# New hand-written order for a chunked recurrence and a gated MLP on one core: narrower unit-matrix products, idle products, and other engines for some pieces

## The chip, the cores and the metric

The kernel runs on one core of one Trainium2 chip. Its time is the device time of one execution in microseconds (us); the time quoted is the median of three runs. Six parts of the core matter: PE (TensorE, the matrix products), PEld (the loading of PE's stationary operand, beside the products), DVE (VectorE), ACT (ScalarE), POOL (GpSimd), and SP, which only issues DMAs. Each works through its own instructions in program order and waits on the others by semaphores.

## The reference

Two parts stand one behind the other. The first is a recurrence over 768 time steps, for 4 batches and 8 heads of width 40:

```
for t in range(S):
    y[:, :, t] = einsum('bhd,bhde->bhe', r_t, state)
    Sa = einsum('bhde,bhe->bhd', state, a_t)
    state = state * w_t - outer(Sa, b_t) + outer(v_t, k_t)
```

The second takes the result as x (4 x 768 x 320) through a gated MLP:

```
h = gelu(x @ w_in)                       # 320 -> 1024
u, v = h[..., :512], h[..., 512:]
v = layernorm(v) * g_ln
v = einsum('ts,bsd->btd', w_sg, v) + b_sg # 768 x 768
out = x + (u * v) @ w_out
```

Everything is in float32; products that need more than one pass split an operand into a high and a low part (names ending in h and l: `vh`, `vl`, `wsh`, `wsl`, `woh`, `wol`, `xh`, `xl`).

## The kernel before

**The recurrence.** The 768 steps are cut into 12 chunks of 64. Inside a chunk the steps are solved together: the decay products and scaled keys are formed for each batch b (the "gates": `ex`, `hs`, `kb`, `at` on DVE and POOL, the products `ab` on PE, the copies `nts`, `kbt`, `at` on ACT), and a triangular system per head pair has to be inverted. The inversion of a chunk is a chain of 58 small operations on POOL (`tg<-x,n`, then `x<-x,tg`), each of which needs the one before. It starts from `n` (a DVE transposition of `nts`) and `x` (an ACT copy of a unit start). Behind it DVE turns the result (`x1z`, later `xt`), PE and ACT finish the inverse (`gp`, `gs`, `xp`), and the chunk's products follow: `ru` (state and right-hand sides), `sp` (the new state), `ut`, `pq` (scores), `yp` (output), which DVE and ACT move on (`rhsb`, `s`, `vu`, `vut`, `vs`, `sc`, `pqs`, `yt`). The chunk's state update `sp` adds the old state through a product with a unit matrix (`sp<-sc,ident`), followed by 16 products of the update itself. The loop runs ahead: while PE works on chunk c, POOL inverts c+1 and the gates of c+2 and c+3 are formed.

For chunk 0 the inversion is divided: DVE does one half of the heads' rows (`tv<-x,n`) and POOL the other (`tg<-x,n`, 15 wide and narrower), both beside the gates of chunk 1.

**The MLP.** Its weights arrive as 64-bit numbers and are taken apart into a high and a low part of 32 bits (`stg`, `lt`, `sc`, then `wih` and `wil`, or `woh` and `wol`): some integer operations on DVE, copies on ACT, and three last operations, "a trio" (`lt<-lt,sc`, `stg<-stg,wih`, `wil<-stg,lt`), on DVE or POOL. The input weights' part of this is laid into the last chunks of the recurrence. Its pieces are named x (load and split of the input, `split_x`), v and u (the two halves of the first product, PE `hv` and `hu`, then a gelu on ACT and DVE and, for v, the norm), s (the product with `w_sg`, PE `sg<-wsh,vh`, `sg<-wsl,vh`, `sg<-wsh,vl`), o (the output product, PE `op`) and j (idle products that nobody reads).

**What sets the order.** Nothing is scheduled by a planner at build time. Every operation goes through `InOrder` (line 146), which pins it to its place in the program, and the places come from tables of numbers at the head of the file. A pair (position, function) is put in a list, the list is sorted by position, and the functions are called in that order: `merge` for chunk 0 and the start of chunk 1, `half` for each half chunk, with 28 units of position to a chunk. The tables that the text below speaks of are `E0K` and `E1K` (one letter for each batch: whether `kb` of chunk 0 and 1 is formed on DVE, V, or on POOL, G), `JUNK` (position and number of idle products in the recurrence), `DEC` (position and engine of the 12 splits of the input weights), `SEQ0`, `SEQ` and `SEQL` (the order of the MLP's pieces), `SGS` and `OUTS` (at which piece each twelfth of `w_sg` and eighth of `w_out` is split), and `SGE` and `OUTE` (on which engine its low part is formed). Since all operations are recorded through `InOrder`, each carries that one line, L156, in the profile; groups are told apart by their tiles.

Of the kernel before, what the change touches and what calls it, by code (L numbers as in the profile page):

```python
# [19 lines left out]
NP = H // 2  # L20
# [16 lines left out]
WARM = (14, 0)  # L37
T0 = 7.22
T1 = 17.01
T2 = 3.25  # L40
TX = 17.22
ISN = 1
LX = 5.0
LV = 9.0
OSP = 1
AQ = 0
YM = 64
C1 = 15.0
WP = 16.0
W16 = 0.42  # L50
K16 = 0
TB0 = 1.08
TB1 = 14.03
CUT0 = ()
HALF = 8
ROWS0 = (6, 31)
T3 = 11.26
T4 = 17.06
CH = ((1.42, 2.46, 7.0, 6.4, 3.47, 7.1, 8.16, 11.36, 3.3, 9.55, 13.14, 14.55), (-0.02, 1.21, 7.67, 4.93, 8.92, 5.92,
    10.0, 10.59, 3.23, 7.11, 13.11, 13.9))  # L60
GPOS = (((0.01, 0.33, 0.61, 1.31, 3.87, 4.25, 4.26, 4.27, 0.611), (2.52, 2.51, 2.79, 3.49, 5.81, 6.43, 6.44, 6.45,
# [10 lines left out]
E1K = "VGGG"
BACK = (17.23, 23.44, 29.46, 23.45)
GX = (24.18, 4.36)
# [17 lines left out]
SEQ0 = (("x0", 0), ("v0", 0), ("v1", 0), ("v2", 0), ("u0", 0), ("x1", 0), ("u3", 0), ("u1", 0), ("u2", 0), ("v3",  # L92
# [4 lines left out]
XL = 2  # L97
REST = 9
SGS = (2, 6, 3, 5, 8, 10, 10, 13, 14, 13, 14, 13)
OUTS = (11, 12, 12, 14, 15, 18, 19, 18)  # L100
XE = "VVVVVVVVVVVV"
UE = "VVVVVVVV"
OSTEP = (-2, 0, 0, 0, 0, 0)
SGE = "VGGGGVGVGVGG"
OUTE = "GGGGGGGG"
SECOND = (17.5, 0.25)
ZERO = (-1, 12.33)
LAST = 2
# [3 lines left out]
MK = 40  # L112
JUNK = ((317.32, 3), (348.72, 4))
TP = 1
UT = 0
GL = (0.01, 0.01)
LAG = ((1.42, 2.31, 0.69, 0.01, 0.01, 1.54, (0.01, 0.69, 0.6, 0.61), (1.29, 1.3, 0.58, 1.19), 2.82, 0.22, 0.11,
    1.02), (0.01, 0.01, 0.88, 0.27, 0.2, 0.01, (0.01, 0.02, 0.35, 0.36), (0.19, 0.3, 0.06, 1.38), 0.01, 0.25, 0.06,
    0.01))
SEQL = ("s1", "s2", "s0", "s3", "s4", "s5", "s6", "s7", "o0", "o1", "o2", "o3", "o5", "o4")  # L120
ROWS = (12, 26)
EX = ((0.01, 0, 0.3, 0.52, 1.42, 2.52, 2.53, 3.02, 0.301), (0.01, 0, 0.3, 0.93, 2.14, 3.24, 3.25, 3.83, 0.54))

# [46 lines left out]
def attention(tc, a, xd, flag, keep, ps, mlp=None):  # L170
# [4 lines left out]
    with ExitStack() as ctx:  # L175
# [463 lines left out]
        def chain3(c, b):  # L639
# [185 lines left out]

        def load_x0():
            Q.dma_start(out=x0, in_=a["x0"])

        def load_v():
            for f in (load_vb, load_vu):  # L830
                for k in range(2):
                    f(0, k)

        bl = blanks()
# [6 lines left out]
              spread(steps16(0, 1, G, K16, 8, "tg"), T3, T4),  # L841
              [(TX + W16 * k, f) for k, f in enumerate(back)], [(LX, load_x0), (LV, load_v)],
              [(C1, lambda: [f() for b in range(2) for f in chain1(0, b)]), (WP, lambda: warmup(WARM[1]))],
# [5 lines left out]

        plan = []  # L850
        for c in range(1, NCH):
# [40 lines left out]
class Mlp:  # L892
# [127 lines left out]

    def weights_rest(self):
        def part_sg(k, c):
# [29 lines left out]
        order = [(k, c) for c in range(2) for k in range(6)]  # L1052
        loads = [lambda x=x: load_sg(*x) for x in order]
        parts = [lambda x=x: part_sg(*x) for x in order]
        wo = [part_out(k, c) for c in range(2) for k in range(4)]
# [108 lines left out]

    def outp(self, b, m, n):
        r = 128 if m < 2 else 64
        mc = slice(128 * m, 128 * m + r)
        self.outs[b, n] = self.outs.get((b, n), 0) + 1
        assert all(("wo", i) in self.ready for i in range(8))
        k = OSP if (b == B - 1 and self.outs[b, n] == 3 and self.outs.get((b, 1 - n)) == 3) else 1  # L1170
        w = 384 // k
        for j in range(k):
            self.outp_part(b, m, n, slice(w * j, w * j + w), w, r, mc)

    def outp_part(self, b, m, n, part, w, r, mc):
        V, Q, sb = self.V, self.Q, self.pr
        c = slice(384 * n + part.start, 384 * n + part.stop)
        o = self.ps("op")[:, 0:w]
        ops = []
        for f in range(4):  # L1180
            h, l = (y[:, part] for y in self.gs[b, f, n])
            if m < 2:
# [18 lines left out]

    def side(self, c, hf):
# [5 lines left out]
        if self.plan is None:  # L1208
# [53 lines left out]
    def run(self, ahead, verdict=None):  # L1262
# [3 lines left out]
        if not ahead:  # L1266
# [143 lines left out]
```

## Time and profile before

| | |
|---|---|
| three runs | 636.78, 638.65, 639.47 us; median 638.65 |
| profiled execution | 635.31 us, span from first to last instruction 633.1 us |
| granted TensorE clock, mean | 0.937 of 2.4 GHz |
| PE busy | 579.1 us, 91% |
| DVE, ACT, POOL busy | 490.2, 392.1, 385.9 us (77%, 62%, 61%) |

The profile's page cuts the span into 40 slices and gives each engine's busy share in tenths, the granted clock and the DMA share:

```profile
PE   6658899999999999999978899598999999999995
DVE  7858788988889888898768778888787769568632
ACT  6928697987978879788765746543454345224410
POOL 7568787888888888888886244566442432343230
PEclk9556699999999999999979899799999999999999
```

A slice is 15.8 us. The recurrence takes the first 24 slices, the MLP the rest. PE is not full in the first five slices, in slices 21 to 23 and in slice 26, and the granted clock is low in about the same places. "Idle before" in a row of the timeline is the time in which the engine had nothing to run, and the name behind the arrow is what it then got.

### The profile page before, as it was taken

How to read it: one execution, taken by the hardware profiler on the slowest of the kernel's cores; microseconds unless marked ns; L12 is line 12 of the kernel's file. 1: busy time of each engine (PE TensorE's matmuls, PEld its weight loads, DVE VectorE, ACT ScalarE, POOL GpSimd, SP SyncE). 2: the span in 40 equal slices, each digit the busy share in tenths (PEclk: the TensorE clock that was granted, in tenths of full speed). 3: DMA queues.
4: the chain of work that ended last, by engine and by line, in shares of the span. 5: the costliest groups of instructions: out<-in, count | busy, mean ns of one | idle time of the engine just before them, and what ended most of it. 6: DMA issues, size and time to landing. Idle time of an engine off the chain costs nothing.

```text
span 633.1 us, 24077 instructions
## 1 busy us (share of the span) xinstructions
PE 579.1 (91%) x9837; PEld 514.9 (81%) x9837; DVE 490.2 (77%) x1074; ACT 392.1 (62%) x1113; POOL 385.9 (61%) x853
## 2 busy tenths in 40 slices
PE   6658899999999999999978899598999999999995
PEld 5556788888888888888867788487899989999995
DVE  7858788988889888898768778888787769568632
ACT  6928697987978879788765746543454345224410
POOL 7568787888888888888886244566442432343230
PEclk9556699999999999999979899799999999999999
DMA  5433233444334444333443325320003103010002
GB/s 197 141 68 94 66 109 105 121 123 124 108 102 123 109 138 108 105 97 94 129 115 101 102 76 170 98 68 10 32 7 100 32 1 107 1 32 14 19 1 68
DMA packets 56887, 54.02 MB, mean 85 GB/s; under 512 B 35840, under 2 KB 47360, under 8 KB 56768
## 3 DMA queue, kind: packets, MB, share of 16 engines
q1 hardware_dynamic: 56768, 52.40, 29.1%
q8 instruction: 79, 1.29, 0.8%
q14 instruction: 40, 0.33, 0.2%
HBM read 44.52 MB, written 7.86 MB: 83 GB/s over the span
## 4 chain that ended last, share of the span: by engine, by line
PE 43%; ACT 21%; DVE 15%; POOL 10%; issue 8%; DMA 2%; SPq 0%; ACTq 0%; POOLq 0%; DVEq 0%
PE sg L156 12%; PE op L156 5%; ACT nts L156 5%; PE hv L156 4%; POOL x L156 4%; POOL tg L156 4%; PE hu L156 4%; PE yp L156 4%; PE ab L156 3%; ACT junk L156 2%; ACT at L156 2%; PE sp L156 2%; PE ru L156 2%; ACT xt L156 2%; PE pq L156 2%
## 5 line engine op out<-in xcount | busy, mean ns | idle before, releaser
L156 POOL TENSOR_TENSOR x<-x,tg 128x126 f32<-128x126 f32 (+24 forms) x334 | 128.5, 385 | 26.1
L156 POOL TENSOR_TENSOR tg<-x,n 128x126 f32<-128x126 f32 (+24 forms) x334 | 122.0, 365 | 32.7 <-ACT x L156 4.0
L156 PE MATMUL sg<-wsh,vh 128*128 128x384 f32 x192 | 66.4, 346 | 4.9 <-ACT vh L156 4.2
L156 POOL TENSOR_TENSOR gx<-g,gy 128x384 fp32r<-128x384 f32 x30 | 32.0, 1073 | 62.7 <-ACT gy L156 62.7
L156 PE MATMUL sg<-wsl,vh 128*128 128x384 f32 x192 | 66.2, 345 | 2.1 <-POOL wsl L156 1.4
L156 PE MATMUL sg<-wsh,vl 128*128 128x384 f32 x192 | 66.1, 344 | 0.8 <-POOL vl L156 0.8
L156 ACT ACTIVATE nts<-ab 32x256 f32<-32x256 f32 x192 | 62.0, 323 | 2.8 <-DVE at L156 0.2
L156 PE MATMUL pq<-rt,vut 128*64 128x128 f32 x768 | 55.7, 289 | 0.2 <-ACT gs L156 0.2
L156 ACT CAST gy<-g 128x384 fp32r<-128x384 f32 x30 | 15.4, 514 | 55.3 <-DVE g L156 52.6
L156 PE MATMUL yp<-pqs,kbt 128*64 128x64 f32 x768 | 46.5, 225 | 2.4 <-DVE pqs L156 0.6
L156 PE MATMUL ab<-at,kb 64*64 64x64 f32 x1536 | 38.8, 243 | 9.9 <-POOL kb L156 4.2
L156 PEld LDWEIGHTS pq<-rt,vut 128*64 128x64 f32 x768 | 44.1, 144 | 3.1 <-DVE lt L156 0.7
L156 ACT CAST vh<-v 128x512 fp32r<-128x512 f32 x24 | 14.9, 620 | 51.2 <-DVE v L156 51.2
L156 PEld LDWEIGHTS ab<-at,kb 64*64 64x64 f32 x1536 | 31.7, 151 | 16.0 <-POOL kbt L156 5.5
L156 POOL TENSOR_TENSOR rs<-rs,mhalf 128x1 f32<-128x1 f32 x24 | 13.7, 571 | 48.6 <-DVE rs L156 40.9
L156 PE MATMUL yp<-rt,s 80*40 80x64 f32 x704 | 42.6, 219 | 0.1
L156 PEld LDWEIGHTS yp<-pqs,kbt 128*64 128x64 f32 x768 | 37.1, 136 | 6.4 <-ACT kbt L156 2.1
L156 PEld LDWEIGHTS sg<-wsh,vh 128*128 128x128 f32 x192 | 37.1, 193 | 6.0 <-ACT vh L156 4.5
L156 POOL TENSOR_TENSOR vl<-v,vh 128x512 fp32r<-128x512 f32 x24 | 31.4, 1311 | 17.3 <-ACT vh L156 17.3
L156 DVE TENSOR_TENSOR pqs<-pq,mask 128x512 f32<-128x512 f32 x48 | 32.0, 682 | 10.1 <-PE pq L156 10.1
L156 PEld LDWEIGHTS sg<-wsl,vh 128*128 128x128 f32 x192 | 37.0, 193 | 3.1 <-POOL wsl L156 1.9
L156 PE MATMUL ru<-rhsb,xt 64*64 64x40 f32 x768 | 32.6, 235 | 7.3 <-ACT xt L156 6.1
(164 smaller groups left out, 1655.4 us busy)
## 6 DMA issues: line engine op xcount, KB each, us to landing
main<-main SPq DMA_DIRECT2D x88, 160.8 KB
vs<-vb SPq DMA_DIRECT2D x24, 160.0 KB
vu<-vs SPq DMA_DIRECT2D x24, 160.0 KB
rt<-rt SPq DMA_DIRECT2D x48, 80.0 KB
vut<-vt SPq DMA_DIRECT2D x24, 160.0 KB
xd<-yt SPq DMA_DIRECT2D x96, 40.0 KB
xt<-xd SPq DMA_DIRECT2D x16, 192.0 KB
out<-y SPq DMA_DIRECT2D x16, 192.0 KB
```

Of the source, the lines that this page charges most:

```text
L156: return self.tc.keep_in_program_order(f(*a, **k))
```

## The change

The file is the same program with other tables and a few other statements:

- The unit-matrix product in `sp` is issued in two parts of 80 columns for each half of the partitions in place of one of 160 (the loop in `chain3`), so 8 instructions in place of 4 for each of the 44 state updates.
- `HEAT` puts 11 products of a constant tile with itself (`wp<-warm`, 128 x 128, 22 instructions) in chunk 0, and `JUNK` has seven entries (29 idle products) in place of two (7). A piece `j6` (six idle products) stands in `SEQ0` ahead of `s1`.
- `wsh` and `wsl` move from the pool `mlp_rest` to a pool of their own, `mlp_sg`, on the other side of the memory, opened at position 313.1. `SGA` is empty, so `early_sg` runs nowhere.
- `E1K` goes from VGGG to GGGV: of chunk 1's four `kb`, the first goes from DVE to POOL and the last from POOL to DVE.
- `SGE` gives DVE six of twelve low parts of `w_sg` in place of four, `OUTE` two of eight of `w_out` in place of none, and `DEC` one more trio of the input weights.
- All other tables have new numbers. The switches `OSP` and `AQ` go; they had the values that leave the program as it is now written. `HALF`, `CUT0` and `ROWS0` are read nowhere.

The core of the difference:

```
-ISN = 1
-E1K = "VGGG"
+E1K = "GGGV"
+HEAT = ((13.17, 11),)
-JUNK = ((317.32, 3), (348.72, 4))
+JUNK = ((294.28, 5), (295.93, 4), (307.25, 6), (312.36, 3), (312.43, 1), (346.91, 3), (349.9, 4))
-SGE = "VGGGGVGVGVGG"
-OUTE = "GGGGGGGG"
+SGE = "GGGGGVGVVVVV"
+OUTE = "VVGGGGGG"
-EARLY = 5
+EARLY = 4
-XL = 2
+XL = 4
-    0), ("v4", 0), ("v5", 0), ("x0", 1), ("u4", 0), ("u6", 0), ("u5", 0), ("u7", 0), ("s1", 0), ("x1", 1), ("s2",
+    0), ("v4", 0), ("v5", 0), ("u4", 0), ("u6", 0), ("u5", 0), ("u7", 0), ("j6", 0), ("s1", 0), ("x0", 1), ("s0",
...
-                w = NP // ISN
-                for g in range(ISN if IS else 0):
+                for g in range(2 if IS else 0):
                     for h in range(2):
                         r = slice(64 * h, 64 * h + 64)
-                        T.matmul(sp[r, w * D * g:w * D * g + w * D], lhsT=ident[:, r],
-                                 rhs=sc[:, w * g:w * g + w].rearrange("p q x -> p (q x)"), start=not g, stop=True,
+                        T.matmul(sp[r, 2 * D * g:2 * D * g + 2 * D], lhsT=ident[:, r],
+                                 rhs=sc[:, 2 * g:2 * g + 2].rearrange("p q x -> p (q x)"), start=not g, stop=True,
...
-        plan = []
+        plan = [(p, lambda k=k: warmup(k)) for p, k in HEAT]
...
+            at(PSG, self.open_sg)
...
     def open_rest(self):
         self.pr = p = self.pool("mlp_rest", "left")
-        self.wsh, self.wsl = (p.tile([128, 6, S], F32R, name=n) for n in ("wsh", "wsl"))
```

What the new numbers move shows best in the instructions of an engine. First POOL at the start of the program, from the last gates of chunk 1 to the first step of chunk 0's inversion (`at_165` and `at_166` belong to batches 2 and 3 of chunk 1). Before:

```order
L156 TENSOR_TENSOR at_165<-main_94,ex_149 128x4x64 [waits DMAHW1_49,DMAHW0_49,DVE_49]
L156 MEMSET kbt_107 128x24
L156 TENSOR_TENSOR kb<-main_94,hs 128x2x4x64 [waits DVE_49,PE_49]
L156 MEMSET kbt_108 128x24
L156 TENSOR_TENSOR at_166<-main_95,ex_150 128x4x64 [waits DMAHW3_49,DMAHW2_49,DVE_49]
L156 MEMSET kbt_109 128x24
L156 TENSOR_TENSOR kb<-main_95,hs 128x2x4x64 [waits DVE_49,PE_49]
L156 MEMSET kbt_110 128x24
```

And in the changed kernel:

```order
L157 TENSOR_TENSOR at_165<-main_94,ex_149 128x4x64 [waits DMAHW1_49,DMAHW0_49,DVE_49]
L157 MEMSET kbt_107 128x24
L157 TENSOR_TENSOR kb<-main_94,hs 128x2x4x64 [waits DVE_49,PE_49]
L157 MEMSET kbt_108 128x24
L157 TENSOR_TENSOR at_166<-main_95,ex_150 128x4x64 [waits DMAHW4_49,DMAHW3_49,DVE_49]
L157 MEMSET kbt_109 128x24
L157 MEMSET kbt_110 128x24
L157 MEMSET kbt_111 128x24
```

The `kb<-main_95,hs` of batch 3 no longer stands between POOL and the chain; DVE has it inside its own half of the inversion (`kb<-main_95,fixed_91`). In exchange POOL has a `kb<-main_92,hs` further up.

Second, PE in chunk 0's second half, at the second `ut` (`ab_1371`, in the changed kernel `ab_1386`, are gate products of chunk 3). Before:

```order
L156 MATMUL sp<-sc_128,ident 64x160 x2
L156 MATMUL sp<-vu_138,kbt_105 40x40 x8
L156 MATMUL ut<-ident,vu_138 80x64 x4
L156 MATMUL ru<-vs_121,at_161 64x40 x8
L156 MATMUL ab_1371<-at_171,kb 64x64
```

And in the changed kernel:

```order
L157 MATMUL sp<-sc_128,ident 64x80 x4
L157 MATMUL sp<-vu_138,kbt_105 40x40 x8
L157 MATMUL ut<-ident,vu_138 80x64 x4
L157 MATMUL wp<-warm 128x128 x11
L157 MATMUL ru<-vs_121,at_161 64x40 x8
L157 MATMUL ab_1386<-at_171,kb 64x64
```

The 11 products stand ahead of the `ru` and of the gate products of chunk 3; the unit-matrix product is twice as many instructions of half the width.

Third, DVE in the first pass of the MLP, between the norms of the last v pieces of batch 0 (`mv`, `rs` are the mean and scale of a norm). Before:

```order
L156 TENSOR_SCALAR v<-v,mv,rs 128x512
L156 BN_AGGR mv<-bs 128x2
L156 TENSOR_SCALAR rs<-mv 128x1
L156 TENSOR_TENSOR xl<-xt_7604,xh 128x384 x2
L156 TENSOR_TENSOR xh<-xt_7604,xh 64x384
L156 SCALAR_TENSOR_TENSOR q<-p,hu 128x384
L156 SCALAR_TENSOR_TENSOR v<-q,hv 128x512
```

And in the changed kernel:

```order
L157 TENSOR_SCALAR v<-v,mv,rs 128x512
L157 BN_AGGR mv<-bs 128x2
L157 TENSOR_SCALAR rs<-mv 128x1
L157 SCALAR_TENSOR_TENSOR q<-p,hu 128x384
L157 SCALAR_TENSOR_TENSOR v<-q,hv 128x512
L157 BN_STATS bs<-v 128x6
```

The split of the next batch's input (`xl`, `xh` from `xt_7604`; `xt_7682` in the changed kernel) has left this place; it comes 38 rows further down, behind two trios of `w_out` and three low parts of `w_sg`.

## Rows read from the trace of the kernel before

**Rows 1.** Stretches: length, busy us (instructions) of PE, PEld, DVE, ACT, POOL; granted clock

```profile
64.60:68.00 3.40, 2.13 (x56) 1.75 (x56) 2.19 (x3) 3.27 (x12) 1.93 (x7) 1.00 0.47 145
68.00:78.30 10.30, 9.85 (x134) 8.38 (x134) 7.54 (x16) 5.40 (x18) 7.79 (x23) 0.50 0.17 51
100.00:300.00 200.00, 195.75 (x5288) 166.65 (x5286) 169.83 (x379) 168.94 (x535) 165.76 (x438) 1.00 0.41 112
380.00:446.00 66.00, 54.86 (x276) 48.85 (x271) 53.80 (x114) 33.22 (x82) 40.56 (x50) 0.92 0.28 83
402.50:412.80 10.30, 7.91 (x21) 6.60 (x22) 6.64 (x14) 5.21 (x14) 6.75 (x7) 0.50 0.37 110
412.83:419.63 6.80, 6.80 (x41) 6.80 (x41) 5.79 (x13) 3.10 (x9) 4.00 (x5) 1.00 0.33 104
446.00:626.00 180.00, 179.58 (x990) 172.65 (x989) 126.10 (x250) 67.85 (x136) 59.23 (x61) 1.00 0.11 34
```

**Rows 2.** Waits of POOL from 82 to 340 us: in total, times, longest

```profile
POOL tg L156 <- ACT x L156: 2.2, 1, 2.2
```

**Rows 3.** Timeline of POOL at the start: start, duration, operation, idle before

```profile
26.52 1.19 POOL L156 TENSOR_TENSOR kb<-main,hs 128x512 f32<-128x512 f32 x1 [3.92 <-DVE x L156]
...
27.99 0.21 POOL L156 TENSOR_TENSOR tg<-x,n 128x15 f32<-128x15 f32 x1
```

**Rows 4.** Timeline of DVE at the start

```profile
15.17 0.69 DVE L156 TENSOR_TENSOR kb<-main,fixed 128x512 f32<-128x512 f32 x1
...
24.90 0.23 DVE L156 SCALAR_TENSOR_TENSOR x<-n,x 128x15 f32<-128x15 f32 x1 [0.89 <-ACT x L156]
...
37.52 1.05 DVE L156 STREAM_TRANSPOSE x1z<-x 128x512 f32<-128x512 f32 x1 [3.04 <-POOL x L156]
```

**Rows 5.** Timeline of PE: the constant products at the start (6.20: a window's part)

```profile
1.13 5.97 PE L156 MATMUL wp<-warm 128*128 128x128 f32 x28 [1.13 <-DVE warm L156]
...
6.20 0.90 PE L156 MATMUL wp<-warm 128*128 128x128 f32 x5
```

**Rows 6.** Timeline of PE in chunk 0 and 1

```profile
64.86 0.66 PE L156 MATMUL ru<-vs,at 64*64 64x40 f32 x16
...
66.92 0.69 PE L156 MATMUL ab<-at,kb 64*64 64x64 f32 x30 [1.27 <-ACT kbt L156]
...
81.03 1.15 PE L156 MATMUL yp<-pqs,kbt 128*64 128x64 f32 x32
```

**Rows 7.** Timeline of PE in a middle chunk, the state update

```profile
131.43 0.49 PE L156 MATMUL sp<-sc,ident 128*64 128x160 f32 x4
131.75 0.47 PE L156 MATMUL sp<-vu,kbt 128*40 128x40 f32 x16
```

**Rows 8.** Timeline of POOL: first steps of two inversions, and the last of chunk 11's

```profile
282.35 0.24 POOL L156 TENSOR_TENSOR tg<-x,n 128x31 f32<-128x31 f32 x1
...
308.70 0.24 POOL L156 TENSOR_TENSOR tg<-x,n 128x31 f32<-128x31 f32 x1
...
337.14 0.28 POOL L156 TENSOR_TENSOR x<-x,tg 128x45 f32<-128x45 f32 x1
```

**Rows 9.** Timeline of DVE behind chunk 11's inversion

```profile
344.39 0.68 DVE L156 TENSOR_TENSOR pqs<-pq,mask 128x512 f32<-128x512 f32 x1
344.99 0.69 DVE L156 STREAM_TRANSPOSE xt<-x1z 128x512 f32<-128x512 f32 x1
...
350.45 0.42 DVE L156 TENSOR_TENSOR lt<-lt,sc 128x256 f32<-128x256 f32 x1 [0.90 <-ACT lt L156]
```

**Rows 10.** Waits of PE from 380 to 446 us, the longest

```profile
PE sg L156 <- ACT vh L156: 4.2, 1, 4.2
```

**Rows 11.** Timeline of PE and DVE in the MLP's first pass

```profile
377.29 1.08 PE L156 MATMUL idle<-wih 128*128 128x512 f32 x4
...
396.27 2.85 DVE L156 TENSOR_TENSOR xl<-xt,xh 128x384 fp32r<-128x384 f32 x2 [0.82 <-ACT xh L156]
...
405.90 1.31 DVE L156 TENSOR_TENSOR wsl<-ws,wsh 128x384 fp32r<-128x384 f32 x1 [1.10 <-ACT wsh L156]
```

More of the change, by code (lines that the diff above doesn't have):

```diff
@@ L37 @@
 WARM = (14, 0)
-T0 = 7.22
-T1 = 17.01
+T0 = 7.27
+T1 = 16.98
 T2 = 3.25
-TX = 17.22
-ISN = 1
[L43 to L46, printed above, removed]
-YM = 64
-C1 = 15.0
-WP = 16.0
-W16 = 0.42
+TX = 17.74
+LX = 2.88
+YM = 64
+HEAT = ((13.17, 11),)
+LV = 7.67
+C1 = 15.05
+WP = 16.2
+W16 = 0.27
 K16 = 0
@@ L53 @@
 TB1 = 14.03
[L54 to L60, printed above, removed]
+CUT0 = (2,)
+HALF = 9
+ROWS0 = (0, 26)
+T3 = 11.21
+T4 = 15.34
+CH = ((0.45, 2.04, 5.42, 6.21, 1.13, 7.18, 8.59, 11.36, 3.3, 10.06, 13.31, 14.77), (0.21, 1.37, 6.72, 4.0, 8.34,
+    5.6, 9.88, 10.86, 3.24, 6.16, 13.32, 13.76))
 GPOS = (((0.01, 0.33, 0.61, 1.31, 3.87, 4.25, 4.26, 4.27, 0.611), (2.52, 2.51, 2.79, 3.49, 5.81, 6.43, 6.44, 6.45,
@@ L71 @@
 E1A = "GGGG"
[L72 to L74 removed]
+E1K = "GGGV"
+BACK = (17.21, 22.21, 30.49, 23.63)
+GX = (24.18, 3.53)
 CG = 0.7978845608028654
@@ L824, in both @@
                     (at + w * (len(first) + 1), lambda: [f() for f in steps(c, n, 31 - LAST, G, (0, 16), "tg")])]
[L826 to L832, printed above, removed]
         bl = blanks()
@@ L841, in attention @@
               spread(steps16(0, 1, G, K16, 8, "tg"), T3, T4),
-              [(TX + W16 * k, f) for k, f in enumerate(back)], [(LX, load_x0), (LV, load_v)],
+              [(TX + W16 * k, f) for k, f in enumerate(back)],
+              [(LX, lambda: Q.dma_start(out=x0, in_=a["x0"])), (LV, lambda: [f(0, k) for f in (load_vb, load_vu) for k in range(2)])],
               [(C1, lambda: [f() for b in range(2) for f in chain1(0, b)]), (WP, lambda: warmup(WARM[1]))],
@@ L931, in pairs, with open_sg, early_sg, load @@
         return [[p.tile([128, HF], F32R, name=f"v{x}{i}") for x in "hl"] for i in range(lo, hi)]
+    def open_sg(self):
+        p = self.psg = self.pool("mlp_sg", "right")
+        self.wsh, self.wsl = (p.tile([128, 6, S], F32R, name=n) for n in ("wsh", "wsl"))
+    def early_sg(self, i):
+        k, c = i % 6, i // 6
+        f = slice(384 * c, 384 * c + 384)
+        z = {}
+        def load():
+            t = z[0] = self.psg.tile([128, 384], F32, name="wt", bufs=1)
+            self.Q.dma_start(out=t, in_=self.wst[128 * k:128 * k + 128, f])
+        def high():
+            self.A.copy(out=self.wsh[:, k, f], in_=z[0])
+        def low():
+            self.pick(SGE, i).tensor_tensor(out=self.wsl[:, k, f], in0=z[0], in1=self.wsh[:, k, f].bitcast(F32), op=ALU.subtract)
+            self.ready.add((k, c))
+        return load, high, low
     def open_rest(self):
         self.pr = p = self.pool("mlp_rest", "left")
-        self.wsh, self.wsl = (p.tile([128, 6, S], F32R, name=n) for n in ("wsh", "wsl"))
         self.woh = p.tile([128, 4, DM + 64], F32R, name="woh")
@@ L1052, in weights_rest @@
         order = [(k, c) for c in range(2) for k in range(6)]
-        loads = [lambda x=x: load_sg(*x) for x in order]
-        parts = [lambda x=x: part_sg(*x) for x in order]
+        loads = [(lambda x=x: load_sg(*x)) if x not in done else None for x in order]
+        parts = [(lambda x=x: part_sg(*x)) if x not in done else None for x in order]
         wo = [part_out(k, c) for c in range(2) for k in range(4)]
@@ L1165, in outp @@
     def outp(self, b, m, n):
+        V, Q, sb = self.V, self.Q, self.pr
+        c = slice(384 * n, 384 * n + 384)
         r = 128 if m < 2 else 64
         mc = slice(128 * m, 128 * m + r)
+        o = self.ps("op")[:, 0:384]
         self.outs[b, n] = self.outs.get((b, n), 0) + 1
         assert all(("wo", i) in self.ready for i in range(8))
[L1170 to L1178, printed above, removed]
         ops = []
         for f in range(4):
-            h, l = (y[:, part] for y in self.gs[b, f, n])
+            h, l = self.gs[b, f, n]
             if m < 2:
@@ L1190, in one @@
             x = self.xts[b % 2, n]
-            y = sb.tile([128, 384], F32, name="y", bufs=2)[0:r, 0:w]
+            y = sb.tile([128, 384], F32, name="y", bufs=2)[0:r]
             if m < 2:
-                V.tensor_tensor(out=y, in0=o, in1=x[:, m, part], op=ALU.add)
+                V.tensor_tensor(out=y, in0=o, in1=x[:, m], op=ALU.add)
             else:
-                V.tensor_tensor(out=y, in0=o[64:128], in1=x[64:128, m, part], op=ALU.add)
+                V.tensor_tensor(out=y, in0=o[64:128], in1=x[64:128, m], op=ALU.add)
                 V.tensor_tensor(out=y, in0=o[0:64], in1=y, op=ALU.add)
-            q = self.A if AQ and b == B - 1 and sum(self.outs.get((b, k), 0) for k in range(2)) == 6 else Q
-            q.dma_start(out=self.out[b, mc, c], in_=y)
+            Q.dma_start(out=self.out[b, mc, c], in_=y)
         self.product(ops, (0, 6, one))
@@ L1225, in side, with sg @@
                 at(PX1, lambda: self.load_x(1, 0))
+            at(PSG, self.open_sg)
+            held = {}
+            def sg(i, j):
+                if not j:
+                    held[i] = self.early_sg(i)
+                held[i][j]()
+            for i, p in SGA:
+                for j, d in enumerate(SGD):
+                    at(p + d, lambda i=i, j=j: sg(i, j))
             for p, k in JUNK:
@@ L1282, in run @@
                 jobs.append((i, lambda: self.later((8, 9, verdict()))))
-        rest, loads, parts, wo = self.weights_rest()
+        rest, loads, parts, wo = self.weights_rest([(i % 6, i // 6) for i, _ in SGA] if ahead else [])
         jobs += [(REST - 3, rest[0]), (REST, rest[1])]
         for k, f in enumerate(loads):
-            jobs.append((SGS[k - 5] if k > 4 else 0, f))
+            if f:
+                jobs.append((SGS[k - 5] if k > 4 else 0, f))
         for k, f in enumerate(parts):
-            jobs.append((SGS[k], f))
+            if f:
+                jobs.append((SGS[k], f))
         for k, g in enumerate(wo):
```

36 lines of the change are left out of this document (20 added, 16 removed), and 6 rows, old and new, of the table SEQ0.

## The prediction

> **What bounds the kernel now.** I read the busy shares by stage first [rows 1], then who waits in each stage, then the timelines at the places that the order changes.
>
> From 446 to 626 us PE is busy for 179.58 of 180 us at the full clock [rows 1]: nothing but fewer products shortens this stage, and the change leaves its products as they are. What can move the end lies before 446.
>
> From 82 to 340 us POOL has one wait in all, 2.2 us for ACT's copy x [rows 2]; otherwise it runs one inversion behind the other, 26.35 us from first step to first step [rows 8]. PE looks just as full there, 195.75 of 200 us, but the reader should see that DVE, ACT and PE each have some rest and POOL's chain, where each step needs the last, has none. So POOL's chains pace chunks 3 to 11, and a microsecond by which they start earlier goes through to 337 us.
>
> From 380 to 446 us PE is busy for 54.86 of 66 us: 11.1 us idle, with a wait of 4.2 us for one `vh` as the longest [rows 1, 10]. In 402.5 to 412.8 the granted clock is 0.50, the lower of the two levels (1.2 of 2.4 GHz), behind that wait [rows 1]. DVE is the busiest there beside PE (53.80 us).
>
> **The start of the first inversion.** POOL stands 3.92 us ahead of `kb` of batch 3, forms it in 1.19 us, and its first step follows at 27.99 [rows 3]. That step needs only `n` and `x`, and DVE's own first step, which needs the same two, ran at 24.90 [rows 4]. With `kb` on DVE POOL can start 3.1 us earlier. Its chain ended 3.04 us behind DVE's half, at about 37.5: DVE waited for it before `x1z` [rows 4]. What is late next is DVE's half: it ended at 37.52 - 3.04 = 34.48 and now holds `kb`, 0.69 us [rows 4], so `x1z` comes at 35.2 in place of 37.52: **-2.3 us**. The most is POOL's own -3.1, the least nothing: ACT and PE feed chunk 2's inversion from the stretch that follows, and if something there doesn't move along, POOL waits longer and the gain is gone. The `kb` that POOL gets in exchange (1.19 us) stands where POOL waits for DVE anyway; without that cover it costs its 1.19.
>
> **The constant products in chunk 0.** The 22 instructions stand behind the second `ut`, ahead of `ru` at 64.86 and of the gate products that waited 1.27 us for ACT [rows 6]. At the start of the program 28 of them took 5.97 us, 213 ns each; the last five in 0.90 us, 180 ns with the end counted in [rows 5]. So 22 cost at most 4.7 us; half of that, 2.4, is what they would take if the start ran at the lower level, which I estimate from the halving of the clock. They fill the 1.27 us. Behind them, from 68.0 to 78.3, PE is busy for 9.85 of 10.3 us at a clock of 0.50, after a stretch at 1.00 with only 2.13 of 3.4 us busy [rows 1]. If PE no longer rests there and the clock stays up, that work takes about 4.9 us less. On PE that is -1.3 - 4.9 + 2.4 to 4.7, so -3.8 to -1.5. What counts is the one gap of POOL that lies behind it, 2.2 us before chunk 3's inversion; more can't be won, since POOL is back to back from there. I take **-1.5 us** of it, since ACT has to follow; bounds -2.2 and, if the products run slow and the clock falls all the same, +3.4 (4.7 less the 1.27 covered).
>
> **Narrower unit-matrix products.** 4 of 160 columns take 0.32 us, from 131.43 to 131.75 [rows 7], 80 ns each; 64 columns take 1.15/32 = 36 ns [rows 6]. Eight of 80 columns lie between 0.29 and 0.64 us; on the line between the two prices it is 43 ns each, 0.34 us, 0.02 more per update, 0.1 per chunk. PE's rest in a chunk, 4.25 us in 200 or 0.56 in 26.35 [rows 1], covers it: **0**. Without cover the upper end is +0.32 for each of 44 updates; that is a rival below.
>
> **Idle products in the recurrence.** 22 more, 0.27 us each by the four in 1.08 us [rows 11]: 5.9 us on PE, from position 294 on, while POOL's last chains set the time. PE's tenths in the page's slices 21 to 23 are 7, 8, 8 (in the section on the profile) and leave between 6 and 11 us of rest, so **0**; if they came where PE is the one waited for, or cold, it would be up to twice 5.9.
>
> **Chunk 11's inversion.** It takes 28.7 us, from 308.70 to 337.14 and 0.28 more, against 26.35 for the one before [rows 8], while DVE works on the input weights. The change gives DVE one more trio, three operations of 0.42 us [rows 9], in that stretch; POOL's own of the same kind stood behind its chain. Bounds 0 and +1.3; I take **+0.5**.
> The longer chain agrees with a rule of the Trainium skill ("SBUF — State Buffer", section "Who interferes with whom"): a DVE instruction with two inputs in SBUF and a GpSimd instruction that reads SBUF exclude each other, and the later one waits for the whole of the earlier. By that rule each of the three could hold POOL for its full length, +1.3, and the sum below would come out 0.8 us later; by the row, where not every one of them meets a step of the chain, less.
>
> **Behind the last inversion.** `xt` stood behind a `pqs` of 0.68 us, 344.39 to 344.99 [rows 9], and now stands ahead of it: **-0.6 us**. ACT's copy of `xt` waited for nothing else there; bounds -0.6 and 0.
>
> **The MLP's first pass.** PE's 4.2 us [rows 10] end with a `vh` that hangs on DVE, and DVE was at the split of the next input, 2.85 us [rows 11] and a smaller `xh` behind it, just ahead of that v. Both now come later than the v, so the wait shrinks to about 1; `j6` (1.6 us) now lies ahead of the s piece and fills that. If PE then keeps the clock, the 21 products of the cold stretch, 7.91 us, run at the pace of 6.80/41 = 0.17 us [rows 1], 3.5 us: 4.4 less. Against it stands work that DVE gets: two low parts of `w_sg` at up to 1.31 us [rows 11] and two trios at 3 x 0.42, up to 5.1 us, in a stage where it is busy for 53.80 of 66 us. Best: -3.2 - 4.4 = -7.6; worst: the wait returns elsewhere and DVE's 5.1 us less its share of rest lands on PE, about +1. I take **-2.5**: the first wait -3.2, `j6` beyond what it fills +0.6, half of the clock's part -2.2, half of DVE's new work +2.5, which makes -2.3, and a little for the shorter queue on POOL.
>
> **The sum** is -2.3 - 1.5 + 0.5 - 0.6 - 2.5 = -6.4 us. On the profiled execution, 635.31 us (span 633.1 and 2.2 around it), that gives 628.9. The median of the runs is 638.65, 3.3 us above it, and I carry the difference over: 632.3.
>
> **The rivals.**
> 1. Only the start counts: the gap before chunk 3 stays, since ACT's copy x hangs on ACT and not on PE, and in the MLP DVE's new work eats the wait that goes. For it: DVE is nearly as busy as PE in 380 to 446. Against: its two operations ahead of that v are plainly gone. 638.65 - 2.3 = 636.4.
> 2. The MLP's gaps close: of 11.1 us of idle time and 4.4 of slow clock two thirds go, 10.3, less `j6` 1.6: -8.7 in place of -2.5, so 6.2 more. For it: the splits of `w_out` and `w_sg` all come earlier. Against: DVE's load. 626.1.
> 3. Slower: the narrow products cost as much as the wide. 36 updates in chunks 3 to 11 at +0.32 are 11.5 us, less 9 x 0.56 of rest, +6.5; the eight in chunks 1 and 2, half of them at the slow clock, about +4, where PE has no rest. PE takes POOL's place as the pace: 632.3 + 10.5 = 642.8. It beats the gain from 0.2 us per update on. For it: each of the eight loads its own stationary operand, twice the loads, and PEld is busy for 166.65 of 200 us. Against: products of 64 columns with the same 64-wide load run every 36 ns.
> 4. The constant products run slow and the clock falls all the same: +3.4 in place of -1.5. For it: 68.0 to 78.3 was slow though PE was 96% busy. 637.2.
>
> **How the numbers follow.** Forecast 42% (its own range 628.5 to 635.4, from its bounds), rival 1 24%, rival 2 15%, rival 3 9%, rival 4 10%. The range reaches down into rival 2 and up past rivals 1 and 4, and leaves out most of rival 3 and the far end of rival 2: 625 to 641. A difference below 0.5%, 3.2 us, can't be told from none here. Under 635.46 lie nearly all of the forecast, rival 2 and a third of rival 1: 0.62. Above 641.84 lie rival 3 and the ends of 4 and 1: 0.11. The rest, 0.27, is the same.
>
> **What would show it.** Start: POOL's first step near 25, `x1z` near 35, with the wait before it on DVE's side small. Constant products: 22 in 2.4 to 4.7 us, clock at 1.00 behind them, and the one POOL wait before chunk 3 under 1 us. State update: 0.3 to 0.4 us for the eight. POOL's other chains every 26.35 us as before, chunk 11's within 30. MLP: PE's longest wait after 380 under 2 us and the clock up from 402 on. The prediction is wrong if the chunks in the middle change their pace, if chunk 2's inversion starts no earlier than before, or if DVE's busy time in the MLP's first pass comes close to its length and PE waits for it.

## The result, and the profile after

The changed kernel takes 620.98 us, the median of four runs (620.27 to 622.11), against 637.76 us for the kernel before in the same comparison: a ratio of 0.9757, 95% interval 0.9722 to 0.9792. It is 2.4% faster by the ratio, 16.8 us by the two medians. The forecast was 632.3 with a range from 625 to 641; the direction was right, but the 6.4 us that it gave the change are less than half of what was gained. The profiled execution took 620.27 us, 15.0 below that of before, with a span of 618.5.

Where the 15.0 us went can be read from a few landmarks, each at its place in the two traces (us from the start of the span):

| landmark | before | after | difference | forecast so far |
|---|---|---|---|---|
| `x1z` of chunk 0 | 37.5 | 34.6 | -3.0 | -2.3 |
| first step of chunk 2's inversion | 68.8 | 66.8 | -2.0 | -2.3 |
| first step of chunk 3's | 97.2 | 93.7 | -3.5 | -3.8 |
| first step of chunk 11's | 308.7 | 304.4 | -4.3 | -3.8 |
| its last step | 337.4 | 332.7 | -4.7 | -3.3 |
| last `xp` | 350.8 | 346.2 | -4.7 | -3.9 |
| last `yp` (end of the recurrence) | 380.4 | 374.1 | -6.3 | -3.9 |
| last `op` | 626.3 | 612.8 | -13.5 | -6.4 |
| end of the span | 633.1 | 618.5 | -14.5 | -6.4 |

First POOL in the changed kernel, the rows that answer to [rows 3, 8] (start, duration, operation, idle before):

```profile
24.98 0.21 POOL L157 TENSOR_TENSOR tg<-x,n 128x15 f32<-128x15 f32 x1 [2.23 <-ACT x L157]
...
66.78 0.24 POOL L157 TENSOR_TENSOR tg<-x,n 128x31 f32<-128x31 f32 x1 [2.68 <-ACT x L157]
...
93.69 0.24 POOL L157 TENSOR_TENSOR tg<-x,n 128x31 f32<-128x31 f32 x1 [0.58 <-ACT x L157]
...
304.44 0.24 POOL L157 TENSOR_TENSOR tg<-x,n 128x31 f32<-128x31 f32 x1
...
332.44 0.27 POOL L157 TENSOR_TENSOR x<-x,tg 128x45 f32<-128x45 f32 x1
```

The first step waits for ACT's x alone, 3.0 us earlier. The gap ahead of chunk 3 is 0.58 us in place of 2.2 [rows 2], that ahead of chunk 2 is 2.68. Chunk 11's inversion takes 28.3 us.

PE around the constant products, which answers to [rows 5, 6]:

```profile
63.99 3.66 PE L157 MATMUL wp<-warm 128*128 128x128 f32 x22
...
74.37 0.50 PE L157 MATMUL sp<-sc,ident 128*64 128x80 f32 x8
74.70 0.47 PE L157 MATMUL sp<-vu,kbt 128*40 128x40 f32 x16
```

The 22 took 3.6 us, and eight unit-matrix products of 80 columns take 0.33, from 74.37 to 74.70. The stretches that answer to [rows 1] (length, busy us of PE, PEld, DVE, ACT, POOL, granted clock; the last two numbers are the DMA share and GB/s):

```profile
66.00:78.30 12.30, 12.12 (x324) 10.76 (x323) 8.42 (x20) 8.02 (x25) 9.49 (x27) 1.00 0.21 61
100.00:300.00 200.00, 196.38 (x5463) 170.16 (x5458) 168.41 (x379) 171.23 (x543) 165.68 (x439) 1.00 0.42 114
346.20:374.10 27.90, 27.17 (x432) 22.12 (x432) 24.10 (x57) 16.67 (x45) 8.31 (x11) 1.00 0.34 89
380.00:440.00 60.00, 53.89 (x275) 50.42 (x274) 51.72 (x119) 30.83 (x76) 30.87 (x40) 0.94 0.26 80
397.10:403.90 6.80, 5.98 (x18) 5.59 (x19) 6.38 (x19) 2.53 (x7) 0.99 (x1) 0.50 0.55 154
```

In this profile the clock is at its lower level from 14.8 to 66.0 us and then at its upper one up to 318.6, where before 68.0 to 78.3 ran at the lower. The 22 constant products so began at the lower level and ended at the upper. The middle of the recurrence is as full as it was. The end of the recurrence, 346 to 374, runs at 1.00 throughout. In the MLP a stretch at 0.50 is still there, 6.8 us in place of 10.3. And these are all the waits of PE from 374 us to the end:

```profile
PE sg L157 <- ACT wsh L157: 4.5, 1, 4.5
PE sg L157 <- DVE v L157: 1.2, 1, 1.2
PE sg L157 <- POOL wsl L157: 0.4, 1, 0.4
```

The sum is 6.1 us, against 11.6 us of idle time in the same stretch before. The longest wait is no shorter than the 4.2 us of [rows 10]; it has another name.

### The profile page after: what moved, and what is told of

Read it like the earlier page. It is cut to its first block, busy times and chain, and to the rows that moved or that the text cites. A ratio compares the mean times of both kernels' runs of the same rounds, so it can differ in the third digit from the quotient of the medians.

```text
span 618.5 us, 24511 instructions
## 1 busy us (share of the span) xinstructions
PE 578.4 (94%) x10060; PEld 520.8 (84%) x10060; DVE 487.2 (79%) x1085; ACT 390.9 (63%) x1113; POOL 374.3 (61%) x842
## 4 chain that ended last, share of the span: by engine, by line
PE 50%; DVE 15%; ACT 14%; POOL 9%; issue 6%; DMA 4%; SPq 1%; POOLq 0%; ACTq 0%; DVEq 0%
PE sg L157 13%; PE op L157 6%; PE hu L157 6%; PE hv L157 6%; POOL x L157 5%; POOL tg L157 4%; PE ab L157 4%; ACT nts L157 3%; PE sp L157 3%; PE yp L157 3%; PE ru L157 2%; DVE at L157 2%; DMA main<-main 2%; DVE sc L157 2%; DVE ex L157 2%
## 5 line engine op out<-in xcount | busy, mean ns | idle before, releaser
L157 POOL TENSOR_TENSOR x<-x,tg 128x126 f32<-128x126 f32 (+24 forms) x334 | 126.3, 378 | 26.1
L157 PE MATMUL pq<-rt,vut 128*64 128x128 f32 x768 | 52.9, 281 | 0.0
L157 PEld LDWEIGHTS pq<-rt,vut 128*64 128x64 f32 x768 | 41.8, 139 | 2.3 <-issue 0.7
L157 DVE SCALAR_TENSOR_TENSOR g<-sg,gl,bt 128x384 f32<-128x384 f32 x32 | 19.7, 615 | 25.4 <-PE sg L157 24.4
L157 DVE TENSOR_TENSOR at<-ab,mask 64x256 f32<-64x256 f32 x96 | 35.7, 407 | 4.5 <-PE ab L157 3.9
```

Of the source, the lines that this page charges most:

```text
L157: return self.tc.keep_in_program_order(f(*a, **k))
```

## The experiments

All ratios are against the kernel before, measured on the same chip and beside it. The changed kernel once more (e11) gave 621.08 us, ratio 0.9768 (0.9749 to 0.9788); I take 0.976 for it, and 0.001 is 0.64 us.

> The changed kernel itself once more, as the measure for the others and for how far its executions scatter: 621, all within 620 to 623 if it has one mode only; some at 625 to 630 if the clock of the wide-product kernel's long runs (629.6, 630.1) is also met here.

Its five runs lie between 619.5 and 622.4.

**The MLP's tables.** Four kernels took apart what the MLP's order and letters do: e1 with both of before, e6 with the letters alone, e7 with the order alone, e8 without `j6`.

```
e1: SEQ0, XL, SGS, OUTS, OSTEP, SGE, OUTE as before
e6: SGE = "VGGGGVGVGVGG"; OUTE = "GGGGGGGG"
e7: SEQ0, XL, SGS, OUTS, OSTEP as before
e8: ("u7", 0), ("j6", 0), ("s1", 0)  ->  without the six products
```

> The changed kernel with the MLP's order (SEQ0, XL, SGS, OUTS, OSTEP) and its engine letters (SGE, OUTE) of before, so without j6; everything of the recurrence stays changed. In the changed kernel the stretch from the last yp to the last op went from 245.9 to 238.7 us. Theory A (these tables alone make that): about 246 us in the stretch, 628 us in all. Theory B (the stretch is shorter since it is entered with a warm clock and another state of the buffers): the stretch stays near 239, 621 in all.

> The changed kernel with only SGE and OUTE of before: DVE gives two low parts of w_sg and two of w_out back to POOL. Theory A1 (the order makes the gain, as it puts sg products ahead of the output products): stretch 239 to 241 us, 621 to 623 in all. Theory A2 (the letters make it: PE's waits for POOL's wsl, gx and woh, 2.6 us, return): 242 to 244, 624 to 626 in all. My forecast's step had DVE's new work as a cost: by it this kernel would be faster, 618 to 620.

> The changed kernel with the MLP's order of before and the new letters; without j6. Theory A1: most of the 7.2 us of the stretch are lost, 244 to 246 us in it, 626 to 628 in all, and PE's wait of 4.2 us for vh is back. Theory A2: 240 to 242, 622 to 624 in all.

> The changed kernel without the six idle products ahead of s1. If they only fill a wait (PE waits 1.2 us for v and 4.5 for wsh behind them): same time, the waits 1.6 us longer and the clock lower for longer, 621 to 622. If they are needed to hold the clock: 2 to 3 us longer, 623 to 624. If they are on the path: 1.6 shorter, 619.4.

| kernel | median us | ratio (95%) | last `yp` to last `op` | PE's waits in it |
|---|---|---|---|---|
| before | 637.76 | 1 | 245.9 | 11.6 (idle) |
| e1, both old | 626.16 | 0.9843 (0.9807 to 0.9879) | 244.2 | 10.1 |
| e7, order old | 624.18 | 0.9813 (0.9770 to 0.9857) | 242.0 | 8.4 |
| e6, letters old | 623.39 | 0.9786 (0.9749 to 0.9824) | 240.9 | 8.7 |
| e8, no `j6` | 622.38 | 0.9804 (0.9746 to 0.9863) | 238.8 | 7.5 |
| changed | 620.98 | 0.9757 (0.9722 to 0.9792) | 238.7 | 6.1 |

The waits of PE in the kernel before, behind the 4.2 us for `vh` of [rows 10], are these (0.7 us more are two small ones for `xh` and `u`):

```profile
PE op L156 <- ACT gy L156: 1.8, 1, 1.8
PE sg L156 <- POOL wsl L156: 1.4, 1, 1.4
PE op L156 <- POOL gx L156: 0.8, 1, 0.8
PE sg L156 <- POOL vl L156: 0.8, 1, 0.8
PE sg L156 <- DVE wsl L156: 0.7, 1, 0.7
PE sg L156 <- ACT wsh L156: 0.7, 1, 0.7
PE op L156 <- POOL woh L156: 0.4, 1, 0.4
```

e1 has them back almost one for one: the last one and the two small ones are missing, and `vh` is 3.9:

```profile
PE sg L157 <- ACT vh L157: 3.9, 1, 3.9
PE op L157 <- ACT gy L157: 1.8, 1, 1.8
PE sg L157 <- POOL wsl L157: 1.4, 1, 1.4
```

In e7, with the new letters, POOL's wsl of 1.4 is gone and `gy` is 0.7:

```profile
PE sg L157 <- ACT vh L157: 4.0, 1, 4.0
PE sg L157 <- DVE wsl L157: 1.0, 2, 0.7
PE op L157 <- ACT gy L157: 0.7, 1, 0.7
```

In e6, with the new order, no `op` waits any more, but with the old letters the next input's split (`xh`) comes 2.9 us late:

```profile
PE sg L157 <- ACT wsh L157: 4.5, 1, 4.5
PE hv L157 <- DVE xh L157: 2.9, 1, 2.9
PE sg L157 <- DVE v L157: 0.9, 1, 0.9
PE sg L157 <- POOL wsl L157: 0.4, 1, 0.4
```

So the tables carry 5.5 us of the stretch, 3.3 by the order and 2.2 by the letters, and neither theory has it alone. The wait of about 4 us at the first s pieces stands in every one of them: the new order turned it from `vh` into `wsh`. What went are the waits behind it: `op` for `gy` and `gx`, since the output products now stand in blocks of 24 behind more sg products, and `sg` for POOL's `wsl`, which is gone with the new letters (e7) and with the new order (e6) alike. My forecast counted DVE's new work as a cost; giving it back (e6) makes PE wait longer, not shorter.

What the letters do under the new order shows in DVE's own rows. In e6 POOL forms three `wsl` where DVE splits the next input; in the changed kernel POOL has nothing there, and the same split takes less than half the time:

```profile
411.74 3.88 POOL L157 TENSOR_TENSOR wsl<-ws,wsh 128x384 fp32r<-128x384 f32 x3
412.12 2.65 DVE L157 TENSOR_TENSOR xl<-xt,xh 128x384 fp32r<-128x384 f32 x2
```

```profile
410.18 1.01 DVE L157 TENSOR_TENSOR xl<-xt,xh 128x384 fp32r<-128x384 f32 x2
```

(The first two rows are e6's, the last one is the changed kernel's.) The 2.85 us of `xl` and the 1.31 us of `wsl` in [rows 11] are such long times too, with POOL at work beside them; a `wsl` that DVE forms while POOL rests takes 0.55 us.

Without `j6` the stretch is the same to 0.1 us: PE waits 1.4 us longer for `wsh`. The idle products fill a wait here and bring nothing to it; the stretch at 0.50 is longer without them (10.3 against 6.8 us). The runs of e8, 621.6 to 627.9, don't tell it from the changed kernel.

The same tables alone in the kernel before (e10):

> The kernel before with the new MLP tables alone (SEQ0 with j6, XL, SGS, OUTS, OSTEP, SGE, OUTE). If the 5.5 us belong to the tables whatever the recurrence does: stretch from last yp to last op 240 to 241 in place of 245.9, 5.5 us below the kernel before. If they need the new recurrence: under 3 us gain.

627.09 us, ratio 0.9862 (0.9836 to 0.9888), the stretch 239.7 us: the gain belongs to the tables and doesn't need the new recurrence. By the ratio it is 8.8 us, in the profile's stretch 6.2, more than the 5.3 and 5.5 that e1 gives back; why it is more was not tried.

**The start.** e5 sets `E1K` back.

```
-E1K = "GGGV"
+E1K = "VGGG"
```

> The changed kernel with E1K back at VGGG: POOL forms the last kb of chunk 1 between the gates and the first inversion. By the step of the forecast: POOL's first step near 28 in place of 24.98, x1z near 37.5 in place of 34.56, of which 0.9 is given back at the wait for x ahead of chunk 2: 2.0 us longer, 623. If the new places of the other gates made the gain: first step near 25 to 26, 621 to 621.5.

623.19 us, ratio 0.9809 (0.9780 to 0.9838). POOL's first step stands at 28.2, `x1z` at 37.7, chunk 3's inversion starts at 96.8 and chunk 11's at 307.6, all 3.1 to 3.3 us later than in the changed kernel, and this wait is back on POOL (waits from 0 to 82 us):

```profile
POOL kb L157 <- DVE x L157: 3.9, 1, 3.9
```

The exchange of the two letters is worth 3.1 us in the trace, and nothing of it is given back.

**The constant products.** e2 leaves them out.

```
-HEAT = ((13.17, 11),)
+HEAT = ()
```

> The changed kernel without the 11 constant products in chunk 0. If they gain by the clock as forecast (1.5 us, the gap of POOL ahead of chunk 3's inversion): clock at 0.50 again near 65 to 77 us, that gap near 2.2 us in place of 0.6, 622.5 in all. If the clock holds without them, or the gap hangs on ACT alone: 621 or less, gap under 1.

621.81 us, ratio 0.9789 (0.9749 to 0.9830). In its profile the clock falls again at their place, and the gap ahead of chunk 3's inversion is back:

```profile
66.70:76.90 10.20, 9.32 (x142) 7.99 (x142) 6.92 (x16) 4.62 (x17) 8.40 (x24) 0.50 0.21 61
```

```profile
95.20 0.24 POOL L157 TENSOR_TENSOR tg<-x,n 128x31 f32<-128x31 f32 x1 [1.96 <-ACT x L157]
```

That step comes at 95.2 in place of 93.7: 1.5 us, as forecast. But this is one pair of profiles. In the twelve profiles that have the constant products and the new `E1K` the step comes between 93.2 and 95.3, in e6 and e16 about as late as here, and the intervals of e2 and of the changed kernel overlap; so the size is not shown. What the clock does is: between 67.6 and 80 us, behind the products, it is at the lower level for 9.3 to 12.4 us in the five profiles without them (before, e2, e9, e10, e15), and for 0 to 3.4 us in the thirteen with them. e11, the same kernel as the changed one, has one of the 3.4, from 71.9 to 75.3.

**The idle products of the recurrence.** The seven entries hold 26 products, not 29 as the section on the change says, so 19 more than before. e3 and, in more rounds, e14 keep only the last two entries; e15 puts all seven into the kernel before.

```
-JUNK = ((294.28, 5), (295.93, 4), (307.25, 6), (312.36, 3), (312.43, 1), (346.91, 3), (349.9, 4))
+JUNK = ((346.91, 3), (349.9, 4))
```

> The changed kernel with only the last two of the seven entries of idle products in the recurrence (3 and 4, like before). If the others hold the clock at the end of the recurrence (1.6 us gained between the last xp and the last yp): a stretch at 0.50 near 344 to 348 us, last yp about 1.6 us later, 622.5 in all. If they only cost PE time that is covered: 621, last yp at 374.1. If they cost: 619 to 620.

> The changed kernel with only the last two idle entries, as in e3, more rounds. If the five others hold the clock at the end of the recurrence: runs of two kinds again, near 621.5 and near 627, median 2 to 5 us above the changed kernel's. If chance: 621.

> The kernel before with the changed kernel's seven idle entries alone. If they hold the clock: no stretch at 0.50 between 340 and 375 us, last yp 1.6 to 4 us earlier, 632 to 634.5. If they only fill rest: 636. If they cost: 637 and more.

e3 gave 624.33 us (0.9810, 0.9756 to 0.9863), its runs 621.5 to 627.6; e14 623.74 (0.9797, 0.9749 to 0.9845), from 622.4 to 630.5. The last `yp` of e3's profile comes at 380.2, 6.1 us later than in the changed kernel, though the last `xp` is only 0.3 later. PE waits 1.46 us right behind `xp`, and a long stretch at the lower level follows:

```profile
347.99 0.30 PE L157 MATMUL ru<-rhsb,xt 64*64 64x40 f32 x2 [1.46 <-ACT xt L157]
```

```profile
349.20:362.90 13.70, 13.70 (x184) 11.75 (x182) 8.96 (x20) 5.95 (x20) 2.68 (x3) 0.50 0.40 99
```

In e14's profile it is 6.8 us at 0.50 there and the last `yp` at 376.0. In the changed kernel the four idle products stand in that wait, and the stretch is at 1.00. The other profiles agree: between 334.1 and 375 us all five without the five new entries (before, e3, e9, e10, e14) have a stretch at the lower level, 3.4 to 13.7 us in all, and of the thirteen with them only e12, below. So they hold the clock, if not in every execution, with 2 to 3 us by the medians, whose intervals overlap with the changed kernel's, and 2 to 6 by the traces. In the kernel before (e15) they give 635.68 us, 0.9957 (0.9935 to 0.9980), 2.7 us by the ratio, with 1.00 from 334 to 402 us in its profile. Its profiled execution, 635.40 us, is no shorter than that of before, and its last `yp`, at 381.8, comes no earlier: it entered chunk 3 at 98.3, 1.1 us later, after a longer time at the lower level at the start, and the idle products cost it 2.4 us ahead of the last `xp` (15.8 us behind the last step of the inversion, 13.4 before), of which the stretch from there to the last `yp` gives 1.9 back (27.6 us, 29.5 before). So this one rests on the ratio alone.

**The width of the unit-matrix product.**

```
-                for g in range(2 if IS else 0):
+                for g in range(1 if IS else 0):
...
-                        T.matmul(sp[r, 2 * D * g:2 * D * g + 2 * D], lhsT=ident[:, r],
-                                 rhs=sc[:, 2 * g:2 * g + 2].rearrange("p q x -> p (q x)"), start=not g, stop=True,
+                        T.matmul(sp[r, 0:4 * D], lhsT=ident[:, r],
+                                 rhs=sc[:, 0:4].rearrange("p q x -> p (q x)"), start=True, stop=True,
...
```

> The changed kernel with one unit-matrix product of 160 columns for each half in place of two of 80. Forecast of the step: 0, 620.5 to 621.5. Theory C (the narrower ones shorten PE's work and with it the chunks, 26.35 to 26.15 us each): 0.2 us per chunk longer, 623. If the narrow ones cost: 619 or less.

> The changed kernel with the wide unit-matrix product, as in e4, more rounds. If the width has to do with the long runs: again some at 629 to 630. If those were chance: all within 619 to 623, median 621.

The four wide ones take 0.32 us as the eight narrow ones do:

```profile
74.49 0.49 PE L157 MATMUL sp<-sc,ident 128*64 128x160 f32 x4
74.81 0.47 PE L157 MATMUL sp<-vu,kbt 128*40 128x40 f32 x16
```

e4's profile has chunk 11's first step at 304.5 and the last `op` at 612.8, the changed kernel's own places. Its four runs, though, were 621.2, 621.2, 629.6 and 630.1 (ratio 0.9862, 0.9789 to 0.9935); e12's six lay between 619.7 and 627.3, median 622.56, ratio 0.9748 (0.9711 to 0.9785). e12's profile was of a long run, and shows where the time goes: the idle products are there, PE still waits 1.17 us for `xt` behind them, and then

```profile
351.30:361.60 10.30, 10.30 (x140) 8.59 (x136) 6.09 (x16) 4.01 (x13) 2.71 (x3) 0.50 0.28 78
```

with the last `yp` at 379.4. The product itself costs the same in both widths. That 3 of 10 runs with wide products were above 627 and none of nine of the changed kernel above 622.4 may hang on the width or be chance; e8, with narrow ones, has such a run too (627.9). This stays open.

**Everything named undone.** e9 takes back all of the above at once and keeps the other numbers of the tables and the new pool.

> The changed kernel with every named part undone at once: E1K, the constant products, the five new idle entries, the MLP's order and letters, and one wide unit-matrix product; what stays of the change is the new numbers of the other tables (places of the gates, of the chunk's pieces, of the loads) and the pool for wsh and wsl. Single removals cost 3.1 (E1K), 1.5 to 2 (constant products), 1.6 to 6 (idle products) and 5.5 us (MLP) in their profiles. If these add up and the rest carries the remaining 1 to 3 us: 632 to 635. If the rest carries nothing: 636 to 638. If the parts overlap: below 631.

636.20 us, ratio 0.9979 (0.9944 to 1.0013): what is left of the change moves the time by nothing that can be measured, by the interval between 3.6 us less and 0.8 more. The single removals, by their ratios, are 5.3 us (MLP), 3.1 (`E1K`), 1.9 (constant products) and 2 to 3 (idle products), 13 in all, against 14 for all at once.

**Toward a better version.** PE's longest wait left, 4.5 us for `wsh`, ends with a copy that ACT makes at 396.96 us, behind two others of `wsh` at 395.03. e13 puts two of these three, the wanted one among them, ahead of the last u pieces.

```
-SGS = (3, 6, 4, 5, 11, 10, 10, 13, 13, 13, 14, 14)
+SGS = (3, 6, 4, 5, 8, 8, 10, 13, 13, 13, 14, 14)
-SGE = "GGGGGVGVVVVV"
+SGE = "GGGGGGGVVVVV"
```

(The expectation says that the seventh low part goes to DVE; it stayed on POOL, in e16 too.)

> The changed kernel with the fifth and sixth split of w_sg put ahead of the last u pieces on ACT (SGS, third pair from 11, 10 to 8, 8) and the sixth low part given to POOL, the seventh to DVE. PE's longest wait in the MLP, 4.5 us for ACT's wsh, stands behind a copy that ACT makes at 395.03 though it idles 1.9 us at 389.2. If that copy's place is what PE waits for: wait gone or under 2 us, stretch 235.5 to 236.5 in place of 238.7, 618 us. If v and its low part end last anyway: 238 to 239 and 621.

623.42 us, 0.9810 (0.9792 to 0.9829): worse. The first wait is gone, and a longer one stands further on:

```profile
PE hv L157 <- ACT xh L157: 5.2, 1, 5.2
```

The table also sets when the later parts are loaded, and SP stood in its queue for a buffer, ahead of the loads for the output weights and the next input:

```profile
386.31 8.80 SPq L157 DMA_DIRECT2D ws<-wst  x3
```

e16 leaves the loads where they were.

> As e13 (fifth and sixth split of w_sg earlier on ACT, their low parts' letters exchanged), with the loads of w_sg left at their old places, since in e13 SP stood 8.8 us at a load that had no buffer, with the output weights' and the next input's loads behind it. If the copy's place is what PE waited for: PE's waits after 380 us 3 us or less in place of 6.1, stretch 235.5 to 237, 618 to 619. If the gain only moves to the wait for the next input's split: 238 to 239 and 621.

620.69 us, 0.9724 (0.9690 to 0.9758). PE's waits are 5.2 us, the stretch 238.4:

```profile
PE hv L157 <- DVE xh L157: 1.4, 1, 1.4
PE sg L157 <- POOL vl L157: 1.2, 1, 1.2
PE sg L157 <- POOL wsl L157: 1.2, 1, 1.2
PE sg L157 <- DVE v L157: 1.1, 1, 1.1
PE sg L157 <- ACT vh L157: 0.3, 1, 0.3
```

The 4.9 us at the first s pieces (4.5 and 0.4) became 2.7, but 1.4 came at the next input's split. The interval of e16 overlaps with the changed kernel's, and its runs, 619.7 to 621.4, lie among that kernel's; it is no better version that could be shown.

## Why the prediction was wrong

**The MLP's first pass (-2.5 forecast, -7.2 measured): the step that failed.** Between the last `yp` and the last `op` PE's idle time went from 11.6 to 6.1 us and its busy time down by 1.7, though `j6` adds six products (the row of before first):

```profile
380.37:626.29 245.92, 234.35 (x1250) 221.21 (x1250) 179.53 (x361) 101.08 (x217) 99.72 (x110) 0.98 0.16 47
374.09:612.83 238.74, 232.62 (x1257) 222.16 (x1256) 176.96 (x368) 100.25 (x217) 90.32 (x101) 0.99 0.16 49
```

"The wait shrinks to about 1" (-3.2) did not come true. The last two `vh` came about 4.8 us earlier in the stretch, as I had argued, and PE waited for neither. It waited 4.5 us for the fifth `wsh`, whose copy at 396.96 stands on ACT behind the last `vh` (393.71) and the u pieces that follow it, and 0.4 for its `wsl`: 4.9 us in place of the 6.3 that the four waits there had cost, so -1.4. I followed the one operation that ended the wait and didn't ask what else the same products need. What did go were the 4.4 us of smaller waits further on, at `wsl`, `gy`, `gx` and `woh`, which I had only counted in the sum of idle time; one of 1.2 us stands there now, for DVE's `v` at 434.7. e6 and e7 show that the order and the letters took them away. My +2.5 for DVE's new work was wrong in sign: by e6 it shortens the stretch by 2.2 us. I had priced it at the 1.31 us that a `wsl` took with POOL at work beside it, and DVE had the room, 51.72 of 60 us busy. The clock still falls: the stretch at the lower level has 5.98 us of busy time in place of 7.91, which I estimate at 1 us from the half of either, against the 2.2 of the sum.

**The idle products (0 forecast, -1.6 between last `xp` and last `yp`).** I priced them as work to be hidden and didn't ask what the clock does. The timeline of before had the clue, the lower level from 354.7 to 358.1. Their number was off too, without effect on the 0: 19 more at 0.27 us are 5.1 us, not 22 and 5.9. And **the -0.6 behind the last inversion** was not there: `xt` came 0.6 us earlier as forecast, but the last `xp` ends 13.4 us behind the inversion's last step in both kernels. PE was full there, with six idle products ahead; without them (e3, e14) it is 13.3 and 13.4, so they explain little of it, and the rest stays open.

**The start (-2.3 forecast, -3.0 measured): a size.** The mechanism was right, and e5 shows it. I held DVE's half to be late next by the 0.69 us of its new `kb`; it took 9.3 us with it, against 9.6 without before, and POOL's bound of 3.1 was the one that counted. Ahead of chunk 2 0.9 of it went into a longer wait for x, and came back by chunk 3.

**The constant products (-1.5) and the narrow products (0).** With the constant products the clock does what I forecast, and their 3.6 us lie between my bounds. That the one pair of profiles gives just 1.5 us is luck in part, since the same step scatters by 2 us. The narrow products went as forecast in their durations. Rival 3 falls by e4's durations, rival 4 by the clock behind the constant products.

**Chunk 11's inversion (+0.5, measured -0.4): a false premise.** The trio that DVE has more stands at 357.8 us, 25 us behind the inversion's end. Beside the inversion DVE does the same 54 operations in both kernels (third number, the row of before first):

```profile
308.70:337.42 28.72, 23.47 (x566) 20.64 (x562) 21.89 (x54) 16.75 (x51) 24.24 (x59) 0.88 0.48 129
304.44:332.71 28.27, 24.61 (x557) 21.45 (x555) 22.07 (x54) 17.47 (x51) 23.80 (x59) 0.88 0.39 106
```

All other profiles have 28.3 to 28.4 us here, so the 28.7 of before is the odd one and the 0.4 may be scatter. The rule of the Trainium skill ("SBUF — State Buffer", section "Who interferes with whom"), from which the prediction had up to +1.3, was not put to the test here; the rows of `xl` in e6, 2.65 us beside POOL and 1.01 without, agree with it.

**The rest.** The eight inversions from chunk 3 on gained 0.7 us together, and with the MLP's old tables (e1) the stretch behind the last `yp` is still 1.7 us shorter than before, 1.4 of it in PE's waits; no run here explains either. The tail behind the last `op` is 5.7 us against 6.8; kernels with the same end show 5.5 to 7.3, so this is scatter. And I carried 3.3 us from the profiled execution to the median; after the change that difference was 0.7. This alone is 2.6 of the 11.3 us by which the forecast was off.

## What to carry to other kernels

When an operation that ends a wait is moved, list all that the waiting instruction needs, and see which comes second; the gain may lie in the many small waits behind it. Moving work to the busier engine can pay; before pricing it, look at whether the duration read from the trace was taken with another engine at work beside it. Products that nobody reads are not only cost: place them in the wait behind which the clock falls, and read the granted clock by stretch before pricing them.

## What the runs showed that I had not expected

The clock's rises and falls lie elsewhere from one execution to the next of the same instructions: in the changed kernel's two profiles the first long rise came at 66.0 and 51.4 us. In the profiles of kernels that share the start of the changed kernel, the first long rise came between 50.4 us (e14) and 66.0 (the changed kernel), and chunk 2's inversion started between 66.3 (e1) and 68.1 us (e6). A single fall at the end of the recurrence, as in e12, costs 5 us; so a change that keeps PE from resting there shows in the spread of the runs as well as in the median: 3 us over nine runs of the changed kernel, 6 to 8 over e3's and e14's.
